# Six groups of an inverse transform as pairs of 64-row tiles, with their evictions and the work behind them in a new order

## The chip, the core and the metric

One core of a Trainium2 chip runs the whole program in one launch. The metric is device time in microseconds (us), the median of several executions. A core has TensorE (PE, matrix products, with a queue of its own for weight loads, PEld), VectorE (DVE), ScalarE (ACT), GpSimd (POOL) and SyncE (SP, which issues most of the transfers here). Each works through its own instructions in order and waits for the others by semaphores. Products land in PSUM, which only DVE and ACT empty in this kernel.

## The reference, cut to what matters

```python
def _A_ref(q, k, v, shift_k, ssm_k, ssm_D):       # S = 2048 positions, D = 640 channels
    k_shift = ...                                 # causal 4-tap convolution of k by channel
    kv = k_shift * v
    y = irfft(rfft(kv, 2*S) * rfft(ssm_k, 2*S))[:S]   # long convolution by channel
    y = y + kv * ssm_D
    return q * y
def _B_ref(x, w1, b1, w2):                        # F = 1728
    h = x @ w1 + b1
    return (h * tanh(softplus(h))) @ w2           # mish
x = A_q
h = x + _A_ref(layernorm(x), A_k, A_v, A_shift_k, A_ssm_k, A_ssm_D)
out = h + _B_ref(layernorm(h), B_w1, B_b1, B_w2)
```

Everything is in bfloat16, with accumulation in float32. `B_x` is not used.

## The kernel before, in words

**The stages.** The long convolution is computed with transforms written as matrix products, in two stages forward (`s1`, `s2`), a product of the two spectra on DVE (`pr`), and two stages back (`i1`, `i2`). The channels come in five blocks `dc` of 128. The first inverse stage has 20 groups, `i1pe{dc}_{gi}`. One group is 16 matmuls (L479): for each of eight sub-blocks two accumulating products, whose stationary operand is a 128x128 piece of the spectrum product `KS`, and whose moving operand is one of two 128x128 constant matrices `a12`. A group fills one PSUM tile of 128x1024 float32 (two banks; there are four such tiles, numbered 0 to 3), and `i1ev{dc}_{gi}` empties it into `Z` (L483) with one cast, on ACT or DVE. The stationary piece is read, and its place in `ks` is free, when the group's matmuls are done.

The second inverse stage takes, for each tile `t` of 128 positions out of 16, four matmuls over `Z` (`i2pe{t}`; for tiles 0 to 3 split into `i2a{t}` over blocks 0 to 3 and `i2b{t}` over block 4). `y{t}` casts the result (128x640) into `tt_s[t]`, a slice of `ks`. Then come, by tile:

- `ln1_{t}` on DVE (bn_stats twice, bn_aggr once) and `ln1p{t}` on POOL (three small instructions, L515 to L517): mean and deviation of the input row; `lnx{t}` (ACT or POOL, L524) normalises it. None of these needs the transforms.
- `wb{t}` (DVE, L538): y times the normalised input; `h{t}` (DVE, L540): plus the input; `bn{t}` (DVE) and `pow{t}` (POOL, L549 and L550): statistics of h; `hc{t}` (DVE, L559): normalised h.
- a transpose of `hc{t}`: by PE for tiles 0 and 1 (`trpe{t}`, L569, then a copy `trev{t}` on ACT), by a transposing transfer on SP for the other tiles (`tr{t}`, L573).

The feed-forward part runs in five units of 256, 256, 512, 512 and 512 positions: unit 0 is tiles 0 and 1, unit 1 tiles 2 and 3, unit 2 tiles 4 to 7, unit 3 tiles 8 to 11, unit 4 tiles 12 to 15. `m1pe{u}_{fp}` (L598, L605) is a seventh of the first product of unit u and needs the transposes of all of its tiles; `hb{u}_{fp}` (ACT) applies mish; `m2pe{t}` (L663, L671) is the second product of tile t, `res{t}` (DVE) adds h, and `d_out{t}` (SP) writes the tile out. L671 is a pair of products of 64 rows each, one on the upper and one on the lower half of the array, with results in two PSUM tiles.

**What sets the order.** All operations are emitted in the order of one hand-written list, `ORDER`. A name with `@n` is a product and the PSUM tile that it writes; `:a`, `:d` and `:p` choose ACT, DVE or POOL where there is a choice (an `i1ev` or `y` without a letter runs on ACT, an `lnx` too). There is no other scheduler: each engine gets its instructions in the order of the list, and waits are put in where data, or a place in a buffer, need them.

**Places.** `ks` holds both halves of `KS`: columns 0 to 20479 and 20480 to 40959, each half with 4096 columns a block. In the second half lie, later on, `w2` (9600 columns from 20480) and the slices `tt_s[t]` (640 columns each, from 30720). `d_w2a`, `d_w2b` and `d_w2c` on SP load `w2`; `w2z` (POOL) zeroes two half chunks of it.

Of the kernel before, what the change touches and what calls it, by code (L numbers as in the profile page):

```python
# [44 lines left out]
pr0_0 s2v1pe_32@0 s2v1ev_0 pr3_64 i1pe1_3@2 d_w14 s2v1ev_64 d_w10 i1pe0_2@3 pr3_96 d_w11 s2v1ev_32 d_w12 i1pe0_1@1 pr4_0 d_w13 i1ev1_3 d_t2m i1pe3_3@0
i1ev0_1 pr2_96 i1pe3_1@2 i1ev3_3 pr2_64 i1pe3_0@1 i1ev0_2 i1pe0_3@0 pr2_0 i1ev3_0 i1pe0_0@3 pr2_32 i1ev3_1 i1pe3_2@1 i1ev0_3 pr4_96 i1pe2_0@2 i1ev0_0
pr4_32 i1pe1_0@0 i1ev2_0 i1pe2_2@3 pr4_64 i1ev1_0 i1pe2_1@2 ln1_8 i1ev3_2 i1pe2_3@0 i1ev2_2 ln1_6 ln1p8 i1pe4_3@1 i1ev2_3 ln1_11 i1pe4_0@3 ln1p6
i1ev2_1 i1ev4_3:d i1pe4_2@0 i1ev4_0 lnx6:p i1pe4_1@2 ln1_4 i1ev4_2 ln1p11 i2a1@1 d_w2a i1ev4_1 ln1_14 i2a0@3 d_w2b ln1p4 d_w2c i2b1 ln1_10 i2a2@0 y1
i2b0 i2pe4@2 y0 wb1 i2pe5@1 y4 h1 i2pe8@3 wb0 y5 h0 i2b2 i2a3@2 y8 bn1 i2pe15@1 y2 i2b3 i2pe12@3 bn0 y15 pow1 i2pe13@0 y3 i2pe11@1 pow0 y12 hc1 wb2
trpe1@2 y11 i2pe7@3 hc0 y13 h2 trpe0@1 trev1:a wb3 i2pe6@0 bn2 trev0:a i2pe10@2 y7 m1pe0_3@1 h3 lnx11 pow2 bn3 m1pe0_2@3 y6 hc2 y10 pow3 ln1_7  # L50
m1pe0_1@0 tr2 lnx8 ln1p10 hc3 hb0_3 m1pe0_5@2 wb8 tr3 hb0_2 h8 ln1p7 m1pe0_6@1 ln1_9 hb0_5 m1pe0_4@3 hb0_1 ln1p14 ln1_15 m1pe0_0@2 hb0_6 lnx4 wb6 w2z
m1pe1_0@0 wb11 lnx10 wb4 lnx7:p hb0_4 m1pe1_4@1 ln1_5 ln1p15 hb1_0 m1pe1_5@3 wb7 hb0_0 h4 ln1p5 hb1_4 m1pe1_3@0 bn8 hb1_5 lnx5:p m1pe1_1@2 ln1_13
hb1_3 pow8 m1pe1_2@1 wb5 hb1_1 h6 ln1p9 lnx15 m1pe1_6@3 bn6 hb1_2 h5 i2pe9@0 pow6 hb1_6 bn4 i2pe14@2 lnx9 ln1p13 m2pe0@1 hc6 ln1_12 y9 tr6 y14 lnx13:p
bn5 lnx14 pow4 hc8 h11 pow5 tr8 m2pe1@3 wb14 h7 ln1p12 hc5 hc4 bn7 tr4 lnx12 wb10 pow7 tr5 bn11 m2pe2@0 h10 pow11 bn10 wb13 pow10 hc7 hc11 tr7 wb9
wb15 m2pe3@2 res0 tr11 h9 hc10 d_out0 h14 tr10 h15 res2 bn9 d_out2 m1pe2_3@1 wb12 pow9 bn14 h12 pow14 m1pe2_6@0 hc9 hb2_3 bn15 tr9 hc14 h13 m1pe2_5@1
tr14 hb2_6 bn12 res3 pow12 m1pe2_4@0 res1 d_out3 hb2_5 pow15 hc12 bn13 tr12 m1pe3_0@2 hc15 pow13 hb2_4 tr15 hc13 d_out1 tr13 m1pe2_0@3 hb3_0 m1pe3_2@1
hb2_0 m1pe3_6@0 hb3_2 m1pe2_1@2 hb3_6 m1pe3_5@3 hb2_1 m1pe2_2@1 hb3_5 m1pe3_1@0 hb2_2 m1pe3_3@2 hb3_1 m1pe3_4@3 hb3_3 m2pe4@1 hb3_4 m2pe6@0 m2pe5@2
res4 res6 d_out6 d_out4 m2pe7@3 m1pe4_2@1 res7 res5 d_out7 d_out5 m1pe4_5@0 m1pe4_6@3 hb4_5 hb4_2 m1pe4_4@2 hb4_6 m1pe4_3@0 hb4_4 m1pe4_0@1 hb4_3
m1pe4_1@3 hb4_0 m2pe9@2 hb4_1 m2pe11@0 m2pe8@1 res11 res9 d_out9 d_out11 m2pe10@3 m2pe15a@0 res10 res8 d_out8 m2pe12@2 res15a d_out15a d_out10
m2pe14@3 m2pe13@1 res14 res12 d_out14 d_out12 m2pe15b@0 res13 d_out13 res15b d_out15b  # L60
# [109 lines left out]
def kernel(  # L170
# [88 lines left out]
    def ev(e, o, i):  # L259
        if e == "act":  # L260
            nc.scalar.copy(o, i)  # L261
        else:
            nc.vector.tensor_copy(o, i)  # L263
# [204 lines left out]
    d_t2m = load("d_t2m", t2m_a, dram["t2m"][:, 0:4096], deps=s1v_in(0, 4096))  # L468
    Z = uv[:].rearrange("p (c j n) -> p c j n", c=NDC, n=P)
    for dc in range(NDC):  # L470
        for gi in range(4):
            p_ = pt()

            def pe(e, gi=gi, p_=p_, dc=dc):
                pz = p_.f32().rearrange("p (g n) -> p g n", g=8)
                for dgl in range(8):
                    b, l = dc * 8 + gi * 2 + dgl // 4, dgl % 4
                    for k in range(2):
                        nc.tensor.matmul(pz[:, dgl, :], KS[:, k, b, :, l], a12[:, k, :], start=k == 0, stop=k == 1)  # L479
# [254 lines left out]
```

## Time and profile before

| | |
|---|---|
| time, median of 3 runs | 225.13 us (225.12 to 225.89) |
| span of the profiled execution (first to last instruction) | 223.5 us |
| busy share of PE, DVE, ACT, POOL in that span | 96%, 60%, 59%, 26% |
| granted PE clock | full, throughout |

The span is the profiled execution's own time as far as the profile has it: it gives no other. The 1.6 us between the span and the median lie before the first and behind the last instruction of the engines. In what follows, times within the span count from its start. A row of the timeline merges like instructions that follow one another; its columns are start, time covered, engine, line, operation, result and operands, count, and in brackets the idle time before it and what ended it. Where a row of the chain of waits names a transfer as the releaser, it was inferred from the times.

### The profile page before, as it was taken

To read this page: it belongs to the slowest core of one execution; us is meant where nothing else is said; L and a number is where in the kernel's file an instruction comes from. 1 tells how busy PE (TensorE), PEld (TensorE's weight loads), DVE (VectorE), ACT (ScalarE), POOL (GpSimd) and SP (SyncE) were. 2 spreads that over 40 slices of the span, in tenths; PEclk is the share of its full clock that TensorE was granted. 3 is DMA by queue.
4 is the path that set the end of the run, shared out by engine and by line. 5 is a ranking of instruction groups with operands and counts; after the bars stand their busy time and mean duration, and the time that the engine had idled before them with its cause. 6 is when DMAs were issued, how large, how long until landed. Compare 5 with 4: busy or idle time off the path is not lost.

```text
span 223.5 us, 6119 instructions
## 1 busy us (share of the span) xinstructions
PE 214.0 (96%) x2645; PEld 157.6 (70%) x2650; DVE 133.2 (60%) x232; ACT 133.0 (59%) x182; POOL 58.9 (26%) x120
## 2 busy tenths in 40 slices
PE   7899999999879999889999999999999999999994
PEld 2899999888869999458877644444567444766763
DVE  2776899999989999889878999100002200022122
ACT  2389888999999999999983015565600075200000
POOL 5147620102860005347887523100000000000000
PEclk9999999999999999999999999999999999999999
DMA  5999994372991789303004443500001100010211
GB/s 181 390 413 409 412 374 121 143 239 93 375 415 69 258 331 290 124 0 62 1 0 62 84 123 91 118 0 0 3 0 59 59 3 0 0 56 6 76 54 49
DMA packets 19563, 30.98 MB, mean 139 GB/s; under 512 B 10704, under 2 KB 14928, under 8 KB 18768
## 3 DMA queue, kind: packets, MB, share of 16 engines
q1 hardware_dynamic: 19104, 30.46, 39.0%
q8 instruction: 21, 0.34, 0.7%
q10 hardware_dynamic: 336, 0.12, 0.2%
q14 instruction: 6, 0.05, 0.1%
q0 software_dynamic: 96, 0.00, 0.0%
HBM read 20.42 MB, written 2.62 MB: 103 GB/s over the span
## 4 chain that ended last, share of the span: by engine, by line
PE 70%; DVE 13%; DMA 9%; ACT 4%; issue 2%; SPq 1%; POOL 1%; DVEq 0%
PE ps L663 26%; PE ps L598 25%; DVE ks L461 6%; DMA ks<-in_B_w_dram 4%; DMA ks<-ks 3%; PE ps L396 3%; PE ps L422 3%; ACT uv L261 3%; DMA ks<-in_A_ssm_k_dram 3%; PE ps L341 2%; PE ps L376 2%; DVE ks L263 2%; PE ps L357 2%; DVE ra L362 1%; PE ps L397 1%
## 5 line engine op out<-in xcount | busy, mean ns | idle before, releaser
L620 ACT ACTIVATE ks<-ps,b1s 128x512 bf16<-128x512 f32 (+1 forms) x69 | 36.1, 610 | 42.8 <-PE ps L598 30.3
L663 PE MATMUL ps<-ks 128*128 128x320 bf16 (+2 forms) x420 | 58.4, 299 | 0.0
L598 PE MATMUL ps<-G 128*128 128x512 bf16 (+1 forms) x320 | 57.0, 336 | 0.3
L688 DVE TENSOR_TENSOR rb<-ps,rb 128x640 bf16<-128x640 f32 x15 | 11.7, 816 | 68.9 <-PE ps L671 66.5
L663 PEld LDWEIGHTS <-ks 128*128 128x128 bf16 x420 | 40.6, 98 | 17.2 <-issue 1.3
L598 PEld LDWEIGHTS <-G 128*128 128x128 bf16 x325 | 31.3, 98 | 24.4 <-issue 1.1
L261 ACT CAST uv<-ps 128x1024 bf16<-128x1024 f32 x49 | 45.2, 1197 | 0.0
L261 ACT CAST ks<-ps 128x960 bf16<-128x960 f32 (+3 forms) x49 | 39.8, 905 | 8.1 <-PE ps L397 5.0
L461 DVE TENSOR_TENSOR ks<-ks,uv 128x2048 bf16<-128x2048 bf16 x20 | 23.1, 1225 | 0.7 <-DMA ks<-ks 0.7
L422 PEld LDWEIGHTS <-G 128*128 128x128 bf16 x512 | 20.9, 96 | 3.1 <-issue 2.5
L479 PE MATMUL ps<-a_t,ks 128*128 128x128 bf16 x320 | 18.8, 219 | 0.4 <-DVE ks L461 0.3
L479 PEld LDWEIGHTS <-ks 128*128 128x128 bf16 x320 | 18.3, 113 | 0.7 <-DVE ks L461 0.6
L422 PE MATMUL ps<-uv,G 128*128 128x64 bf16 (+1 forms) x384 | 12.8, 186 | 1.8 <-ACT uv L261 1.8
L544 DVE BATCH_NORM_STATS2 st<-rb 128x6 f32<-128x320 bf16 x32 | 14.0, 478 | 0.1
L515 POOL TENSOR_SCALAR ve<-mv 128x1 f32<-128x1 f32 x16 | 4.7, 292 | 34.9 <-DVE mv L511 34.2
L510 DVE BATCH_NORM_STATS2 st<-rb 128x6 f32<-128x320 bf16 x32 | 13.7, 471 | 0.0
L263 DVE CAST uv<-ps 128x1024 bf16<-128x1024 f32 x11 | 12.9, 1204 | 0.1
L362 DVE TENSOR_TENSOR ra<-ps,rb 128x1024 bf16<-128x1024 f32 x10 | 11.9, 1222 | 0.7 <-PE ps L358 0.5
L524 POOL TENSOR_SCALAR ra<-rb,r,nmr 128x640 bf16<-128x640 bf16 x8 | 8.9, 1118 | 10.0 <-PE ps L397 9.3
L422 PE MATMUL ps<-ks,G 128*128 128x160 bf16 x128 | 11.2, 230 | 0.0
L396 PE MATMUL ps<-cst,ra 128*64 128x128 bf16 x160 | 10.6, 219 | 0.7 <-ACT uv L261 0.5
L263 DVE CAST ks<-ps 128x1024 bf16<-128x1024 f32 (+1 forms) x9 | 10.5, 1197 | 0.5 <-PE ps L422 0.3
...
## 6 DMA issues: line engine op xcount, KB each, us to landing
...
```

The lines of the kernel that those rows point to most:

```text
L261: nc.scalar.copy(o, i)
L263: nc.vector.tensor_copy(o, i)
L362: nc.vector.tensor_tensor(kv_w[:, m, :, 8 * h:8 * h + 8, :], p_.f32().rearrange("p (l t d) -> p d t l", l=4, t=8), raw_v[:, 8 * h:8 * h + ...
L396: nc.tensor.matmul(ps[0:64, dgl, :], lhs, mc, start=True, stop=True)
L422: nc.tensor.matmul(p_.f32()[:, o:o + n], g_v[:, f, :], src[:, :, f, :], start=True, stop=True)
L461: nc.vector.tensor_tensor(o, o, v, ALU.mult)
L479: nc.tensor.matmul(pz[:, dgl, :], KS[:, k, b, :, l], a12[:, k, :], start=k == 0, stop=k == 1)
L510: nc.vector.bn_stats(st1[:, t, hh, :], xt(t)[:, hh * 320:(hh + 1) * 320])
L544: nc.vector.bn_stats(st2[:, t, hh, :], xt(t)[:, hh * 320:(hh + 1) * 320])
L598: nc.tensor.matmul(ph[:, o:o + w], w1[:, dc, fc * P:fc * P + P], lt[:, dc, 0:w], start=dc == 0, stop=dc == NDC - 1)
L620: nc.scalar.activation(hb[:, fc, 0:n], p_.f32()[:, i * 512:i * 512 + n], ACT.Mish, bias=b1s[:, fc:fc + 1], scale=1.0)
L663: nc.tensor.matmul(p_.f32()[:, o:o + n], lhs, w2[:, k, cols:cols + n], start=fc == 0, stop=single and fc == 13)
```

## The change

Three things change together.

1. The constant tables are laid out anew, so that the 128 rows of a piece of `KS` fall into two halves of 64 that belong to different channels (two channels out of four each). `a12` then has two 64x64 blocks on its diagonal and zeros elsewhere. For the six groups of `ROW_I1` a matmul of 128 rows by 128 moving columns becomes two of 64 rows by 64 columns, one on each half of the array, which write to the two banks of the group's PSUM tile: 32 matmuls and 32 weight loads in place of 16 and 16. All 20 casts `i1ev` read PSUM in runs of two numbers in place of four.
2. `w2` and the slices `tt_s` change places: `tt_s` now lies where blocks 0, 1 and half of 2 were, `w2` where half of 2, 3 and 4 were. Loading `w2` then needs the last groups of block 4 to be done.
3. `ORDER` is new from the last products `pr` on. The casts of groups 2_1, 4_2, 2_3 and 4_3 go to DVE (before, only that of 4_3). `i1pe1_0` moves behind the groups 2_2 and 2_1, and the order of the last groups is new. The six `ln1` that stood between and behind the last casts (tiles 4, 6, 8, 10, 11, 14) move behind `hc2`, and `y0` goes to DVE. Of the `lnx` from tile 4 on, those of tiles 4, 5, 7, 8, 11, 13 and 15 are on POOL (before 5, 6, 7 and 13), and those of 6, 9, 10, 12 and 14 on ACT. `w2z` moves ahead of `pow1`. The units' tiles come in the order 5, 7, 6, 4, then 8, 10, 9, 11, then the rest; the seven `m1pe2` come ahead of all `m1pe3`; `m2pe15a` is now last but one. Elsewhere PSUM tiles 2 and 3 only swap names.

```diff
+ROW_I1 = "2_1 2_3 4_0 4_1 4_2 4_3".split()
...
-    T["g"] = np.moveaxis(G, 4, 6).reshape(128, 128 * 128)
+    T["g"] = G.reshape(2, 16, 4, 128, 2, 16, 2, 2).transpose(0, 1, 2, 3, 6, 5, 7, 4).reshape(128, 128 * 128)
...
-    a12 = np.stack([np.moveaxis(A1, 0, 2).reshape(128, 128), np.moveaxis(A2, 0, 2).reshape(128, 128)], axis=1)
+    a12 = np.zeros((2, 64, 2, 2, 64))
+    for h in range(2):
+        a12[h, :, :, h] = np.stack([np.moveaxis(a, 0, 2).reshape(64, 64) for a in (A1, A2)], axis=1)
...
-    w2 = ks[:, 20480:20480 + 15 * D].rearrange("p (c d) -> p c d", c=15)
-    tt_s = [ks[:, 30720 + t * D:30720 + (t + 1) * D] for t in range(NT)]
+    w2 = ks[:, 30720:30720 + 15 * D].rearrange("p (c d) -> p c d", c=15)
+    tt_s = [ks[:, 20480 + t * D:20480 + (t + 1) * D] for t in range(NT)]
...
-                pz = p_.f32().rearrange("p (g n) -> p g n", g=8)
+                row = f"{dc}_{gi}" in ROW_I1
+                pz = p_.f32().rearrange("p (h g n) -> p h g n" if row else "p (g h n) -> p h g n", h=2, g=8)
                 for dgl in range(8):
                     b, l = dc * 8 + gi * 2 + dgl // 4, dgl % 4
                     for k in range(2):
-                        nc.tensor.matmul(pz[:, dgl, :], KS[:, k, b, :, l], a12[:, k, :], start=k == 0, stop=k == 1)
+                        for r in [slice(0, 64), slice(64, 128)] if row else [slice(0, 128)]:
+                            o = pz[:, r.start // 64, dgl, :] if row else p_.f32()[:, dgl * P:(dgl + 1) * P]
+                            nc.tensor.matmul(o, KS[r, k, b, :, l], a12[r, k, r], start=k == 0, stop=k == 1)
...
-                ev(e, Z[:, dc, :, gi * 32:gi * 32 + 32].rearrange("p j (g l) -> p j g l", l=4), p_.f32().rearrange("p (g j l) -> p j g l", g=8, l=4))
+                ev(e, Z[:, dc, :, gi * 32:gi * 32 + 32].rearrange("p j (g h l) -> p j g h l", h=2, l=2), p_.f32().rearrange("p (h g j l) -> p j g h l" if f"{dc}_{gi}" in ROW_I1 else "p (g h j l) -> p j g h l", h=2, g=8, l=2))
```

The list from the last products to the first product of unit 0, before:

```
pr4_96 i1pe2_0@2 i1ev0_0
pr4_32 i1pe1_0@0 i1ev2_0 i1pe2_2@3 pr4_64 i1ev1_0 i1pe2_1@2 ln1_8 i1ev3_2 i1pe2_3@0 i1ev2_2 ln1_6 ln1p8 i1pe4_3@1 i1ev2_3 ln1_11 i1pe4_0@3 ln1p6
i1ev2_1 i1ev4_3:d i1pe4_2@0 i1ev4_0 lnx6:p i1pe4_1@2 ln1_4 i1ev4_2 ln1p11 i2a1@1 d_w2a i1ev4_1 ln1_14 i2a0@3 d_w2b ln1p4 d_w2c i2b1 ln1_10 i2a2@0 y1
i2b0 i2pe4@2 y0 wb1 i2pe5@1 y4 h1 i2pe8@3 wb0 y5 h0 i2b2 i2a3@2 y8 bn1 i2pe15@1 y2 i2b3 i2pe12@3 bn0 y15 pow1 i2pe13@0 y3 i2pe11@1 pow0 y12 hc1 wb2
trpe1@2 y11 i2pe7@3 hc0 y13 h2 trpe0@1 trev1:a wb3 i2pe6@0 bn2 trev0:a i2pe10@2 y7 m1pe0_3@1 h3 lnx11 pow2 bn3 ...
```

And after, to the transposes of unit 2:

```
pr4_96 i1pe2_0@3 i1ev0_0
i1pe2_2@0 i1pe2_1@2 pr4_32 i1ev2_0 i1ev3_2 pr4_64 i1ev2_2 i1pe1_0@3 i1pe4_2@1 i1ev2_1:d i1ev1_0 i1ev4_2:d i1pe2_3@0 i1ev2_3:d i1pe4_1@2 i1pe4_3@3
i1ev4_3:d i1ev4_1 i1pe4_0@1 i2a0@2 i1ev4_0 i2a1@0 i2b1 i2b0 i2a2@1 y1 i2b2 i2pe4@3 y0:d wb1 i2pe5@0 i2a3@2 wb0 y2 h1 i2b3 w2z h0 y4 bn1 bn0 i2pe6@1 y5
y3 y6 pow1 wb2 i2pe15@3 i2pe7@0 pow0 hc1 d_w2a i2pe13@2 y15 wb3 hc0 y13 h2 i2pe10@1 bn2 y7 h3 bn3 pow2 pow3 d_w2c i2pe11@3 hc2 tr2 ln1_6 hc3 trpe1@2
ln1_5 ln1_4 ln1_8 ln1p6 y11 i2pe12@0 ln1_7 ln1p5 trev1:a trpe0@3 lnx5:p ln1_10 ln1_15 i2pe8@2 trev0:a y12 y10 m1pe0_4@3 wb5 hb0_4 m1pe0_1@0 hb0_1
m1pe0_6@1 ln1_11 ln1p4 m1pe0_3@3 tr3 ln1p7 d_w2b ln1_13 h5 y8 lnx4:p m1pe0_2@0 hb0_6 ln1_9 ln1p8 wb4 lnx7:p hb0_3 wb7 lnx6 m1pe0_0@2 wb6 bn5 hb0_2 h4
hb0_0 h6 lnx8:p m1pe0_5@1 h7 ln1p15 ln1p11 m1pe1_1@3 bn4 m1pe1_4@0 lnx11:p pow5 wb8 hb0_5 m1pe1_2@2 ln1p9 hb1_1 m1pe1_0@1 hb1_4 wb11 bn7 hb1_2 hb1_0
ln1_14 ln1p10 m1pe1_5@3 m1pe1_3@0 hc5 m1pe1_6@2 i2pe9@1 hb1_5 hb1_3 pow7 bn6 i2pe14@3 pow6 h8 pow4 hc7 tr5 hb1_6 lnx15:p y9 m2pe0@0 bn8 y14 hc6
m2pe1@2 pow8 wb15 tr7 lnx9 hc4 wb9 ln1_12 lnx10 m2pe3@1 tr6 ln1p12 tr4 m2pe2@3 ...
```

More of the change, by code (lines that the diff above doesn't have):

```diff
@@ L45 @@
[L45 to L60, printed above, removed]
+sw2_0 s1vev4_0 s1vev3_3:d sw2_1 s1vpe4_2@0 lnx2:p s1vev4_2 s2v0pe_96@3 pr1_64 ln1p3 s2v0pe_16@2 s2v0ev_96 s2v2pe_32@0 s1vev2_3:d lnx3:p s2v0ev_16
@@ new lines @@
+m1pe0_6@1 ln1_11 ln1p4 m1pe0_3@3 tr3 ln1p7 d_w2b ln1_13 h5 y8 lnx4:p m1pe0_2@0 hb0_6 ln1_9 ln1p8 wb4 lnx7:p hb0_3 wb7 lnx6 m1pe0_0@2 wb6 bn5 hb0_2 h4
+hb0_0 h6 lnx8:p m1pe0_5@1 h7 ln1p15 ln1p11 m1pe1_1@3 bn4 m1pe1_4@0 lnx11:p pow5 wb8 hb0_5 m1pe1_2@2 ln1p9 hb1_1 m1pe1_0@1 hb1_4 wb11 bn7 hb1_2 hb1_0
+ln1_14 ln1p10 m1pe1_5@3 m1pe1_3@0 hc5 m1pe1_6@2 i2pe9@1 hb1_5 hb1_3 pow7 bn6 i2pe14@3 pow6 h8 pow4 hc7 tr5 hb1_6 lnx15:p y9 m2pe0@0 bn8 y14 hc6
+m2pe1@2 pow8 wb15 tr7 lnx9 hc4 wb9 ln1_12 lnx10 m2pe3@1 tr6 ln1p12 tr4 m2pe2@3 wb10 res3 res0 ln1p14 h11 h9 lnx14 res1 lnx12 bn9 h10 hc8 bn10 ln1p13
@@ new lines @@
+bn11 lnx13:p m1pe2_6@1 pow10 wb13 wb14 m1pe2_2@0 pow11 h13 hb2_2 hc10 wb12 h14 pow9 hc9 hc11 tr8 bn13 h12 bn14 m1pe2_3@2 tr10 hb2_6 m1pe2_4@0
+m1pe2_0@1 d_out0 res2 bn12 pow13 h15 hb2_3 m1pe2_5@2 tr11 tr9 hb2_4 bn15 pow12 m1pe2_1@0 m1pe3_5@3 hb2_5 pow15 m1pe3_3@2 d_out1 hc13 hb2_0 m1pe3_2@1
+hb3_5 hc15 hb3_2 m1pe3_0@3 pow14 tr13 hb3_0 m1pe3_6@1 hc12 hb3_6 hc14 m1pe3_1@3 m1pe3_4@1 hb2_1 hb3_4 d_out3 tr15 tr12 m2pe5@0 hb3_1 m2pe7@1 tr14
+m2pe4@3 res7 res5 m2pe6@1 m1pe4_2@0 res4 m1pe4_5@3 res6 hb4_2 m1pe4_4@1 d_out2 d_out7 hb4_4 m1pe4_1@0 hb4_5 m1pe4_6@1 hb3_3 m1pe4_3@3 hb4_1 m2pe9@2
@@ L61 @@
+d_out5 hb4_3 d_out6 m2pe8@0 m1pe4_0@3 hb4_6 m2pe11@1 hb4_0 res11 m2pe12@3 d_out4 m2pe14@1 res9 m2pe10@2 res12 m2pe13@3 res14 res13 d_out12 d_out14
+res10 m2pe15a@1 m2pe15b@3 d_out9 d_out13 d_out10 d_out11 res15a res8 d_out15a res15b d_out8 d_out15b
 """.split()
+ROW_I1 = "2_1 2_3 4_0 4_1 4_2 4_3".split()
 CHUNKS = [[0, 1], [2], [3, 4]]
@@ L144, in _make_tables @@
         G[1, :, dl, :, 1, :, dl] = -c
-    T["g"] = np.moveaxis(G, 4, 6).reshape(128, 128 * 128)
+    T["g"] = G.reshape(2, 16, 4, 128, 2, 16, 2, 2).transpose(0, 1, 2, 3, 6, 5, 7, 4).reshape(128, 128 * 128)
     th = 2 * np.pi * g[:, None] * t2[None, :] / 16
     cg, sg = np.cos(th), np.sin(th)
-    A1 = np.zeros((2, 16, 4, 2, 16, 4))
-    A2 = np.zeros((2, 16, 4, 2, 16, 4))
-    for dl in range(4):
+    A1 = np.zeros((2, 16, 2, 2, 16, 2))
+    A2 = np.zeros((2, 16, 2, 2, 16, 2))
+    for dl in range(2):
         A1[0, :, dl, 0, :, dl] = cg
```

7 lines of the change are left out of this document (4 added, 3 removed).

## The prediction

> **What bounds the kernel now.** I read the table of windows first, cut at the end of the last spectrum product (84.7), the start of the first `y` (about 91.2) and the start of unit 0 (99.5).
>
> ```profile
> 84.70:91.20 6.50, 5.74 (x92) 5.10 (x90) 6.33 (x18) 6.45 (x8) 4.34 (x12) 1.00 1.04 343
> 91.20:99.50 8.30, 7.72 (x63) 4.51 (x63) 7.17 (x19) 7.99 (x14) 2.63 (x6) 1.00 0.03 6
> 99.50:220.60 121.10, 120.78 (x819) 75.11 (x821) 46.73 (x115) 45.20 (x82) 26.15 (x57) 1.00 0.16 40
> ```
>
> Columns: stretch, length, busy time of PE, PEld, DVE, ACT, POOL, then clock and DMA. From 99.5 on PE is busy 120.78 of 121.10 us at full clock, and the change adds or takes no product there. So the end can move by what unit 0's start moves, by any gap that opens later, and by the tail. The stretch from 84.7 to 99.5 decides. Its rows in the timelines of PE, ACT and DVE:
>
> ```profile
> 72.87 16.70 PE L479 MATMUL ps<-a_t,ks 128*128 128x128 bf16 x288
> 91.20 5.33 PE L531 MATMUL ps<-uv,ra 128*128 128x128 bf16 x40 [0.77 <-ACT uv L261]
> 98.11 0.45 PE L569 MATMUL ps<-ident,rw 128*128 128x128 bf16 x5 [0.31 <-DVE rw L559]
> 99.49 14.35 PE L598 MATMUL ps<-G 128*128 128x256 bf16 x130
> ...
> 55.23 35.92 ACT L261 CAST uv<-ps 128x1024 bf16<-128x1024 f32 x39
> 91.51 6.66 ACT L261 CAST ks<-ps 128x640 bf16<-128x640 f32 x11 [0.36 <-DMA ks<-in_B_w_dram]
> 97.94 1.43 ACT L261 COPY G<-ps 128x640 bf16<-128x640 bf16 x2
> ...
> 65.28 19.39 DVE L461 TENSOR_TENSOR ks<-ks,uv 128x2048 bf16<-128x2048 bf16 x17 [0.69 <-DMA ks<-ks]
> 87.61 1.18 DVE L263 CAST uv<-ps 128x1024 bf16<-128x1024 f32 x1
> 88.71 0.88 DVE L510 BATCH_NORM_STATS2 st<-rb 128x6 f32<-128x320 bf16 x2
> 92.31 0.49 DVE L538 TENSOR_TENSOR ks<-ks,ra 128x640 bf16<-128x640 bf16 x1 [0.49 <-ACT ks L261]
> 92.83 0.49 DVE L540 TENSOR_TENSOR rb<-ks,rb 128x640 bf16<-128x640 bf16 x1
> 93.24 0.48 DVE L538 TENSOR_TENSOR ks<-ks,ra 128x640 bf16<-128x640 bf16 x1
> 94.17 0.88 DVE L544 BATCH_NORM_STATS2 st<-rb 128x6 f32<-128x320 bf16 x2
> 95.21 0.83 DVE L544 BATCH_NORM_STATS2 st<-rb 128x6 f32<-128x320 bf16 x2
> 97.61 0.45 DVE L559 TENSOR_SCALAR rw<-rb,mv,r 128x640 bf16<-128x640 bf16 x1 [0.46 <-POOL r L550]
> ```
>
> Products end at 65.28 + 19.39 = 84.67. ACT casts without a break to 55.23 + 35.92 = 91.15, 0.92 us each; PE's groups also take 16.70 / 18 = 0.93, so the two are matched and ACT ends last. PE then waits 0.77 us for ACT and starts `i2b1` at 91.20, and `y1` follows at 91.51. The row of `y1` names the load of `w2`. I don't take it: `i2b1` is two short products from 91.20, and `y1` can't precede them; load or no load, the cast ending at 91.15 is the limit. From there the path is y1, wb, h, bn, pow, `hc0` (97.61), its transpose (98.11), the second copy on ACT (97.94 + 1.43 = 99.37), unit 0 (99.49).
>
> **Part 1, the casts.** Behind its last product DVE now runs the four casts that it gets, with no `ln1` ahead. One takes 1.18, and the next instruction started 1.10 behind it (87.61 to 88.71). The first starts at 84.6, the fourth ends at 84.6 + 3 x 1.10 + 1.18 = 89.1. ACT has three casts fewer: 91.15 - 3 x 0.92 = 88.4 if never starved. New runs of two numbers: DVE's PSUM reader with the longest strides (L362, single numbers) and the plain casts cost the same, so I add nothing.
>
> ```profile
> L263 DVE CAST uv<-ps 128x1024 bf16<-128x1024 f32 x11 | 12.9, 1204 | 0.1
> L362 DVE TENSOR_TENSOR ra<-ps,rb 128x1024 bf16<-128x1024 f32 x10 | 11.9, 1222 | 0.7 <-PE ps L358 0.5
> ```
>
> **Part 2, the pairs.** No row shows a pair of 64 by 64. The nearest are L671's pairs of 64 rows in the chain of waits, and the second forward stage, whose moving operand is short (timeline of PE):
>
> ```profile
> 115.70 10.60 PE ps L663 x78
> 126.30 0.38 PE ps L671 x4
> 126.67 3.64 PE ps L663 x26
> ...
> 60.04 1.58 PE L422 MATMUL ps<-uv,G 128*128 128x64 bf16 x48 [0.28 <-ACT uv L261]
> 70.12 2.79 PE L422 MATMUL ps<-uv,G 128*128 128x32 bf16 x96
> ```
>
> A full matmul of L663 takes 10.60 / 78 = 0.136. Four of L671 as two pairs that share the array would be 0.27, one after another 0.54; 0.38 stands there, so they pair, and 0.11 is the change to halves and back. A matmul of 64 columns takes (1.58 less some 0.16 of drain) / 48 = 0.030. Lower bound: a pair costs one such matmul, 16 x 0.030 = 0.47 a group. Upper bounds: each matmul counts by itself, 32 x 0.030 = 0.95, or at the old pace of 0.93 / 16, 1.86. I take 0.47, since L671's rows show sharing, and 0.1 for each of four changes of form.
>
> PE must also wait for PSUM. Group 2_1 and then 1_0 run while the last product ends; 1_0 waits for the cast of 2_0 in its PSUM tile (eight casts ahead of ACT's last before, 91.15 - 8 x 0.92 = 83.8, and unmoved) and leaves PE at 84.8. Group 4_2 runs at 84.9; 2_3 waits for ACT's cast of 2_2 (the second behind 2_0, at 85.7); then 4_1, 4_3, 4_0 follow: 85.7 + 4 x 0.47 + 0.16 of drain = 87.7. DVE wants 4_3 at 87.9 and gets it at 87.3; ACT casts 4_1 and 4_0 by 88.8. DVE is last, at 89.1 in place of 91.15: **2.05 us won**. By the same steps PE takes over from DVE once a group costs over some 0.6, and each 0.1 more costs about 0.4.
>
> **Part 3, from y to unit 0.** `i2b1` starts at 89.15, `i2b0` right behind it, and its result is there by 89.5. `y0` on DVE is bounded by L688, which reads the same PSUM tile in 0.82 (next row): it ends at 90.35, the `y1` of ACT before that. So `wb1` starts at 90.35 against 92.31. The list interleaves wb1, wb0, h1, h0, so that none waits for the one ahead: 4 x 0.41 (from 92.83 to 93.24) = 1.64, against 94.17 - 92.31 = 1.86. `bn1` starts at 92.0, 2.15 earlier than 94.17. From there to `hc0` the steps are the old ones (bn1, bn0, POOL's pow0; wb2, hc1 and wb3 fit into that wait). Behind `hc0` transpose and copy are the same, and ACT has few enough `y` ahead (10 of 0.6 us from 89.5). Unit 0 starts at 99.49 - 2.2 = **97.3**.
>
> ```profile
> L688 DVE TENSOR_TENSOR rb<-ps,rb 128x640 bf16<-128x640 f32 x15 | 11.7, 816 | 68.9 <-PE ps L671 66.5 <-PE ps L663 2.3
> ```
>
> **Part 4, unit 2 in time?** The `ln1` moved out of the old shadow, and three more `lnx` on POOL, now load DVE and POOL while unit 0 runs. What hides them is PE's work up to `m1pe2`, which started at 130.62 and would start at 128.4. It needs `tr4`, the last of unit 2, issued behind `hc4`; ahead of `hc4` in DVE's queue is `wb15`, which waits for POOL's `lnx15`. POOL's rows between 99 and 128, the transposes' landing and unit 2's start:
>
> ```profile
> L550 POOL TENSOR_TENSOR r<-ve,mhalf 128x1 f32<-128x1 f32 x9 | 5.4, 599 | 0.8
> L516 POOL TENSOR_TENSOR r<-ve,mhalf 128x1 f32<-128x1 f32 x8 | 4.9, 618 | 0.7
> L549 POOL TENSOR_SCALAR ve<-mv 128x1 f32<-128x1 f32 x9 | 3.1, 348 | 4.8 <-DVE mv L545 4.5
> L524 POOL TENSOR_SCALAR ra<-rb,r,nmr 128x640 bf16<-128x640 bf16 x3 | 2.6, 867 | 0.2
> L517 POOL TENSOR_SCALAR nmr<-mv,r 128x1 f32<-128x1 f32 x8 | 2.6, 320 | 0.8
> L515 POOL TENSOR_SCALAR ve<-mv 128x1 f32<-128x1 f32 x8 | 2.1, 258 | 0.3
> ...
> G<-rw SPq DMA_TRANSPOSE x9, 2.6
> ...
> 130.62 3.41 PE L598 MATMUL ps<-G 128*128 128x512 bf16 x14
> ```
>
> One `ln1p` takes 0.26 + 0.62 + 0.32 and some 0.22 between, 1.42; a pow 0.35 + 0.60 + 0.09 = 1.04; an `lnx` 0.95. Up to `lnx15` POOL has nine, four and six of them: 12.8 + 4.2 + 5.7 = 22.7 us. It starts when `ln1_6` is done, some 5 us behind `hc0` (two h, two bn of 1.04, `hc2`, `ln1_6`), at 100.4, and ends at 123.1. `wb15` and `hc4` take 0.9, `tr4` lands 2.6 later, at 126.6. DVE's own work in that time (11 `ln1`, 5 bn at 1.04, 12 wb and h at 0.4, 3 hc) is 22.5 us from 99.4, a little less. So 1.8 us are left, and the move costs nothing; without that cover each us past 128.4 would be a us. Unit 3 gains room, since all of `m1pe2` now stands ahead of `m1pe3`.
>
> **Part 5, places and queues.** `d_w2a` now waits for group 4_0 (87.7) in place of 1_0; nothing queues on SP behind it but `tr2`, issued at 99, and `m2pe0` needs `w2` only 16 us after unit 0's start: no cost. `w2z` on POOL finds it idle (2.63 busy of 8.30). The tail:
>
> ```profile
> 215.04 5.51 PE L663 MATMUL ps<-ks 128*128 128x320 bf16 x42
> 220.58 0.42 DVE L685 TENSOR_TENSOR rb<-ps,rb 128x256 bf16<-128x256 f32 x1 [0.70 <-PE ps L663]
> 221.03 0.33 SPq L692 DMA_DIRECT2D out_dram<-rb  x1
> ```
>
> Behind PE's last product come 0.42 and one write. `res8` (0.82) and its write now stand ahead of them; PE's last product takes 5.51 - 28 x 0.136 = 1.7, `res15a` and `res8` by 0.42 for 256 columns and 0.82 some 1.45, so they fit, with 0 to 0.2 lost.
>
> **Sum.** -2.2 of 223.5: a span of 221.3. The median shown lies 1.63 above the span, and I keep that distance: 225.13 - 2.2 = **222.9**. About 0.5% (1.1 us) is what a measurement of this kernel can tell from no change. The forecast's own range is 222.2 (shorter waits, `y0` at less than L688's time) to 223.7 (a group at 0.7).
>
> **Rival A: halves pair, but each short matmul pays its own floor.** Going from 64 to 32 columns saved L422 next to nothing (0.030 to 2.79 / 96 = 0.029), so a floor per instruction is there. If it holds over both halves together, a group is 0.93. Then 4_2 leaves PE at 85.9, the other four at 89.6, the last cast on ACT ends near 90.8; with the 0.15 of part 3, 0.5 is won: 224.6. For it: that floor. Against it: L671's 0.38, though with 320 columns. The Trainium skill, TensorEngine Tiling (Array Packing), section Instruction Overhead, speaks for this rival: about 60 cycles for each matmul on trn2, and no tiling factor is to be taken from a dimension that is already small. By its figure 32 x 60 cycles, at the 2.4 GHz of the skill's page TensorE: Matmul & The Clock Gate (opening table), would be an estimated 0.8 us a group and about 223.9 in the end; no run here shows it for pairs of 64 columns. Chance 0.15, spread from 223.7 to 225.
>
> **Rival B: unit 2 comes late.** POOL's chain of 22.7 us has a slack of 1.8. Single `ln1p` in the rows above vary (idle 1.8 us over eight, by pieces), and DVE and POOL wait for each other. A tenth more is 2.3 us, a gap of 0.5: 223.4. A fifth more is a gap of 2.7: 225.6, slower than before; this is the way to the other side, and from a chain of 26.7 us on (18% over my sum) the whole gain is gone. Chance 0.15, two thirds of it under 224.0.
>
> **Rival C: halves take turns.** If a 64-row matmul keeps the array for the 0.058 of the old pace, five groups in a row cost 9.3 us, the last cast ends near 95.3, 4.15 late, and the time is some 229. The point from which this is slower is about 1.05 a group. L671 speaks against it. With eviction of short runs going slower (L362 speaks against that) chance 0.08.
>
> **How the numbers follow.** Forecast 0.62, A 0.15, B 0.15, C 0.08. Faster by over 0.5% (under 224.0): 0.62 + 0.04 of A + 0.09 of B = 0.75. Within: 0.11 of A and 0.04 of B = 0.15. Slower by over 0.5%: C and 0.02 of B = 0.10. From 222.2 to 225.0 lie nearly all of the forecast and of A and most of B, a little over 0.8.
>
> **What would show it.** Right: L479's 64-row matmuls at about 0.03 a pair; the last `uv` cast on DVE ending near 89.1; L598's first row near 97.3; PE busy without a gap to about 218.4. Wrong: row groups near 0.9 with PE, not DVE, ahead of the last cast (A); an idle time of PE before unit 2's first L598, with a transposing transfer or POOL behind it (B).

## The result, and the profile after

| | before | after |
|---|---|---|
| time, median | 225.27 us (225.12 to 225.89, 4 runs) | 222.97 us (222.90 to 223.17, 4 runs) |
| ratio | | 0.9889, interval 0.9865 to 0.9914 |
| span of the profiled execution | 223.5 us | 221.2 us |

The forecast was 222.9 with a span of 221.3. The table of windows of the changed kernel, cut at the end of the last spectrum product, the start of `i2b1` and the start of unit 0 (columns as before):

```profile
84.50:89.20 4.70, 4.42 (x172) 3.44 (x169) 4.63 (x5) 4.10 (x5) 1.25 (x2) 1.00 0.04 7
89.20:97.16 7.96, 7.79 (x63) 4.66 (x63) 7.25 (x18) 7.48 (x13) 1.76 (x4) 1.00 0.86 278
97.16:218.30 121.14, 120.74 (x817) 75.16 (x820) 52.53 (x132) 43.23 (x79) 33.22 (x71) 1.00 0.17 40
```

The last stretch is as long as before (121.14 against 121.10) and as full, so all of the gain lies ahead of unit 0. The first stretch was 6.5 us long and is 4.7, the second was 8.3 and is 8.0. The timelines of PE, ACT and DVE in them:

```profile
72.88 15.15 PE L485 MATMUL ps<-a_t,ks 128*128 128x128 bf16 x384
88.18 6.87 PE L537 MATMUL ps<-uv,ra 128*128 128x512 bf16 x48 [0.15 <-DVE uv L266]
97.16 14.35 PE L604 MATMUL ps<-G 128*128 128x256 bf16 x130
...
53.43 33.15 ACT L264 CAST uv<-ps 128x1024 bf16<-128x1024 f32 x36
87.00 2.08 ACT L264 CAST uv<-ps 128x1024 bf16<-128x1024 f32 x2 [0.42 <-PE ps L485]
89.55 6.34 ACT L264 CAST ks<-ps 128x640 bf16<-128x640 f32 x10 [0.47 <-PE ps L537]
...
64.84 19.66 DVE L464 TENSOR_TENSOR ks<-ks,uv 128x2048 bf16<-128x2048 bf16 x17 [0.25 <-DMA ks<-ks]
84.42 4.75 DVE L266 CAST uv<-ps 128x1024 bf16<-128x1024 f32 x4
89.73 0.82 DVE L266 CAST ks<-ps 128x640 bf16<-128x640 f32 x1 [0.56 <-PE ps L537]
90.47 0.88 DVE L544 TENSOR_TENSOR ks<-ks,ra 128x640 bf16<-128x640 bf16 x2
92.08 0.88 DVE L550 BATCH_NORM_STATS2 st<-rb 128x6 f32<-128x320 bf16 x2
95.37 0.45 DVE L565 TENSOR_SCALAR rw<-rb,mv,r 128x640 bf16<-128x640 bf16 x1
```

DVE's four casts follow its last product without a break and end at 84.42 + 4.75 = 89.17; ACT's last ends at 87.00 + 2.08 = 89.08, where it ended at 91.15 before. From the last cast to unit 0 it is 7.99 us in place of 8.34: `wb1` to `bn1` takes 1.61 in place of 1.86, and the other steps are within 0.15 of what they were. Unit 0 starts at 97.16 in place of 99.49.

A ruler for what follows. In every run there is one row of PE that the change does not reach, the last 96 matmuls of the second forward stage; it starts at 70.12 before and at 70.13 after. From its start to unit 0's start it is **29.37 us before and 27.03 after, 2.34 less**. This leaves out small offsets from the start of an execution, which single profiles have (up to 0.8 us below).

### The profile page after: what moved, and what is told of

It is laid out like the page before. It is cut to its first block, busy times and chain, and to the rows that moved or that the text cites. A ratio compares the mean times of both kernels' runs of the same rounds, so it can differ in the third digit from the quotient of the medians.

```text
span 221.2 us, 6309 instructions
## 1 busy us (share of the span) xinstructions
PE 212.5 (96%) x2740; PEld 156.0 (71%) x2746; DVE 137.6 (62%) x236; ACT 127.9 (58%) x175; POOL 62.0 (28%) x123
## 4 chain that ended last, share of the span: by engine, by line
PE 72%; ACT 12%; DVE 6%; DMA 5%; issue 2%; SPq 1%; DVEq 0%; ACTq 0%
PE ps L669 26%; PE ps L604 26%; ACT uv L264 9%; PE ps L537 3%; DMA ks<-ks 3%; PE ps L399 3%; PE ps L425 3%; DMA ks<-in_A_ssm_k_dram 3%; PE ps L344 2%; PE ps L379 2%; DVE ks L266 2%; ACT ks L264 2%; PE ps L360 2%; DVE ra L365 1%; DVE uv L266 1%
## 5 line engine op out<-in xcount | busy, mean ns | idle before, releaser
L669 PEld LDWEIGHTS <-ks 128*128 128x128 bf16 x420 | 40.6, 98 | 17.4 <-issue 1.3
L264 ACT CAST ks<-ps 128x960 bf16<-128x960 f32 (+3 forms) x48 | 39.3, 896 | 8.3 <-PE ps L400 5.0
L264 ACT CAST uv<-ps 128x1024 bf16<-128x1024 f32 x46 | 42.6, 1157 | 0.5 <-PE ps L485 0.4
L485 PE MATMUL ps<-a_t,ks 128*128 128x128 bf16 (+1 forms) x416 | 17.1, 208 | 0.4
L485 PEld LDWEIGHTS <-ks 128*128 128x128 bf16 (+1 forms) x416 | 16.5, 114 | 1.0 <-issue 0.4
L266 DVE CAST uv<-ps 128x1024 bf16<-128x1024 f32 x14 | 16.4, 1210 | 0.2
L530 POOL TENSOR_SCALAR ra<-rb,r,nmr 128x640 bf16<-128x640 bf16 x11 | 12.5, 1133 | 9.9 <-PE ps L400 9.3
L266 DVE CAST ks<-ps 128x1024 bf16<-128x1024 f32 (+2 forms) x10 | 11.3, 1160 | 1.0 <-PE ps L537 0.6
L528 ACT ACTIVATE ra<-rb,nmr,r 128x640 bf16<-128x640 bf16 x5 | 4.5, 925 | 11.9 <-POOL nmr L523 11.9
```

Of the source, the lines that this page charges most:

```text
L485: nc.tensor.matmul(o, KS[r, k, b, :, l], a12[r, k, r], start=k == 0, stop=k == 1)
L669: nc.tensor.matmul(p_.f32()[:, o:o + n], lhs, w2[:, k, cols:cols + n], start=fc == 0, stop=single and fc == 13)
```

## The experiments

| kernel | time, us | ratio to before, interval | ruler, us |
|---|---|---|---|
| before | 225.27 | | 29.37 |
| after | 222.97 | 0.9889 (0.9865 to 0.9914) | 27.03 |
| pairs alone | 225.28 | 0.9992 (0.9974 to 1.0010) | 29.37 |
| places alone | 226.15 (one run) | | 29.37 |
| after, no pairs | 225.12 | 0.9994 (0.9976 to 1.0013) | 28.37 |
| after, casts back on ACT | 224.85 | 0.9984 (0.9957 to 1.0011) | 29.00 |
| after, halves in turn | 224.53 | 0.9963 (0.9951 to 0.9976) | 28.65 |
| after, `y0` on ACT | 223.24 | 0.9905 (0.9884 to 0.9925) | 27.34 |
| after, `ln1_6` ahead | 223.11 | 0.9900 (0.9880 to 0.9920) | 27.32 |
| after, all groups as pairs | 226.61 | 1.0050 (1.0031 to 1.0069) | 31.88 |

Four more runs, on what comes behind unit 0, stand at the end.

**The pairs alone.** Tables and `ROW_I1` of the changed kernel, list and places of the kernel before.

```diff
 (before)
+ROW_I1 = "2_1 2_3 4_0 4_1 4_2 4_3".split()
+... the tables, the matmuls and the casts' runs as in the change
```

> The kernel before, with its own order and places, and only the new tables and the six groups as pairs. Theory: ACT's row of casts up to 91.15 is the bound and doesn't get shorter, so the time is that of before, 225.2 (225.0 to 225.4), with PE idle between the groups. Rival (PE is the bound of the stage): six groups shorter by 0.4 each, 2.4 us, so 222.8 or so.

Measured: 225.28 us. The timeline of PE in this run:

```profile
70.24 2.79 PE L425 MATMUL ps<-uv,G 128*128 128x32 bf16 x96
87.65 0.72 PE L485 MATMUL ps<-a_t,ks 64*128 64x64 bf16 x32 [0.20 <-ACT uv L264]
88.57 0.72 PE L485 MATMUL ps<-a_t,ks 64*128 64x64 bf16 x32 [0.20 <-ACT uv L264]
99.61 1.58 PE L604 MATMUL ps<-G 128*128 128x256 bf16 x13
```

A group is done in 0.72, and the next starts 0.92 behind it, when ACT frees its PSUM tile. A faster PE meets the casts' pace and gains nothing. The new tables and the runs of two numbers cost nothing either.

**The new order without the pairs.**

```diff
 (after)
-ROW_I1 = "2_1 2_3 4_0 4_1 4_2 4_3".split()
+ROW_I1 = []
```

> The kernel after, with all 20 first inverse groups as full 128-row products (ROW_I1 empty); order, places and casts as after. Theory (DVE's casts set the end of the stage only because pairs let PE feed them): five full groups of 0.93 behind the last product end on PE near 89.6, the last cast near 90.8 in place of 89.2, unit 0 starts some 1.5 us later (98.7 in place of 97.2), time 224.5 (224.2 to 224.8). Rival (the gain comes from casts and order alone, PE has room): time within 0.3 of 222.97.

Measured: 225.12 us, above the range of the theory. PE's windows (here instructions of L485 alone: PE, PEld, clock, DMA share), its timeline and ACT's:

```profile
87.40:88.30 0.90, 0.90 (x20) 0.90 (x18) 1.00 0.04 9
...
88.51 1.01 ACT L264 CAST uv<-ps 128x1024 bf16<-128x1024 f32 x1 [1.14 <-PE ps L485]
90.29 1.01 ACT L264 CAST uv<-ps 128x1024 bf16<-128x1024 f32 x1 [0.78 <-PE ps L485]
...
70.91 2.79 PE L425 MATMUL ps<-uv,G 128*128 128x32 bf16 x96
99.28 1.91 PE L604 MATMUL ps<-G 128*128 128x256 bf16 x16
107.03 7.27 PE L604 MATMUL ps<-G 128*128 128x256 bf16 x65 [0.50 <-DMA G<-rw]
```

In the stage itself the theory holds: PE needs 0.90 for a group, both casting engines now wait for it (ACT as shown, DVE 0.34 twice), and the ruler is 28.37, so the pairs are worth 1.34 in this order and the rest of the change 1.00 without them. The miss comes later: at 107.03 PE waits 0.50 us for unit 1's transposes, a wait that neither the kernel before nor the changed one has. In all it is 31.80 us from unit 0 to unit 2's first product in this run, against 31.13 in both of those. What makes those transposes late is shown under the last experiment.

**The casts back on ACT.**

```diff
 (after)
-... i1ev2_1:d ... i1ev4_2:d ... i1ev2_3:d ...
+... i1ev2_1 ... i1ev4_2 ... i1ev2_3 ...
```

> The kernel after, with the casts of groups 2_1, 4_2 and 2_3 on ACT again (4_3 stays on DVE). Theory: ACT has three casts more, three times 0.92, and ends near 91.2 in place of 89.1; 2.0 us later, time 225.0 (224.7 to 225.3). Rival (the pairs bring the gain whoever casts): within 0.4 of 222.97.

Measured: 224.85 us. The timeline of PE:

```profile
69.91 2.79 PE L425 MATMUL ps<-uv,G 128*128 128x32 bf16 x96
90.08 3.15 PE L537 MATMUL ps<-uv,ra 128*128 128x512 bf16 x21 [1.11 <-ACT uv L264]
98.91 2.34 PE L604 MATMUL ps<-G 128*128 128x256 bf16 x20
```

PE is done with the groups early and waits 1.11 us for ACT. Of the 2.34 only 0.37 is left. With the run before: the change without the three shared casts brings 0.37, without the pairs 1.00, with both 2.34. Each of the two removes one of two matched limits, PE and the casts.

**Halves in turn.** The same 32 matmuls of a group, in another order: first the 16 of the upper half, then the 16 of the lower.

```diff
 (after)
-for dgl in range(8):
-    for k in range(2):
-        for r in [slice(0, 64), slice(64, 128)]: ...
+for r in [slice(0, 64), slice(64, 128)]:
+    for dgl in range(8):
+        for k in range(2): ...
```

> The kernel after, with the 32 matmuls of a pair group in another order: all 16 of the upper 64 rows, then all 16 of the lower, so that no two neighbours may share the array. Theory (the short group comes from two halves at work at once, 0.033 a pair): a group takes 32 x 0.030 to 0.033, 0.95 to 1.07, as rival A of the prediction had it; the last cast near 91, time 224.7 to 225.4. Rival (what shortens a group is the number of columns, whatever the neighbours; or the queue brings halves together): 222.97 within 0.3.

Measured: 224.53 us, just under the theory's range. A window of one group in the changed kernel and one in this run (L485 alone), then this run's timeline of PE:

```profile
86.25:86.78 0.53, 0.53 (x43) 0.53 (x39) 1.00 0.00 0
```

```profile
87.65:88.51 0.86, 0.86 (x39) 0.86 (x37) 1.00 0.00 0
...
69.97 2.79 PE L425 MATMUL ps<-uv,G 128*128 128x32 bf16 x96
98.62 2.56 PE L604 MATMUL ps<-G 128*128 128x256 bf16 x22
```

(The counts include matmuls that run over the window's edge.) A group of pairs takes 0.53 us, 0.033 a pair; in turn it takes 0.86, 0.027 a matmul (0.95 to 1.07 was expected for the group). So of the two orders only the one with neighbours on different halves lets the halves work at the same time, and this alone is worth 1.62 of the 2.34. Whether the matmuls themselves or their weight loads are what runs side by side, these two runs don't separate. The price in turn is close to what rival A had for pairs. By the Trainium skill, TensorEngine Tiling (Array Packing), Instruction Overhead, 60 cycles for each matmul made an estimated 0.8 us a group. That agrees with the matmuls in turn (0.86) and not with the pairs (0.53), which behave as if each half paid it by itself.

**`y0` on ACT, and `ln1_6` ahead of `y0`.** Two steps of part 3 undone, one at a time.

```diff
 (after, y0 on ACT)
-y0:d
+y0
 (after, ln1_6 ahead)
-i1ev4_3:d i1ev4_1 ... hc2 tr2 ln1_6 hc3
+i1ev4_3:d ln1_6 i1ev4_1 ... hc2 tr2 hc3
```

> The kernel after, with y0 on ACT in place of DVE. Theory: ACT, which casts y without a break up to the copy of the transposes, gets one more cast of 0.6 ahead of both copies, and DVE wins nothing as wb0 needs y0 anyway; unit 0 starts 0.4 to 0.6 later, time 223.4 to 223.6. Rival (ACT has room there, DVE is the path): DVE has 0.75 less ahead of wb1, time 222.3 to 222.9.

> The statistics of the next tile (ln1_6, three VectorE instructions of about 1.0 together) stand again among the casts at the end of the inverse's first stage, as in the kernel before, behind the last cast that VectorE has there and ahead of y0; all else is as in the changed kernel. Theory: VectorE idles 0.57 ahead of y0 in the changed kernel, so 1.0 there makes y0 and, behind it, wb1, bn1 and unit 0 later by about 0.4: 223.2 to 223.6. Rival: y0 isn't on the path to unit 0 and the statistics are hidden: 222.7 to 223.1.

Measured: 223.24 and 223.11 us. By the ruler, which is 0.31 and 0.29 longer, both directions are right and both sizes too large. The medians are 0.27 and 0.14 longer, which is inside the intervals, and both lie below the theories' ranges, the second at the edge of its rival's. With `y0` on ACT, `wb1` starts no later than in the changed kernel, but ACT's copies of the transposes end later; with `ln1_6` ahead, DVE's idle 0.56 us in front of `y0` takes up half of it.

**The places alone.**

```diff
 (before)
-    w2 = ks[:, 20480:...]   tt_s = [ks[:, 30720 + t * D:...] ...]
+    w2 = ks[:, 30720:...]   tt_s = [ks[:, 20480 + t * D:...] ...]
```

> The kernel before, with only w2 and the slices tt_s changing places, so that the load of w2 waits for group 4_1 (about 89.5 in place of 83.4) and lands 8 us later, near 98. Theory (the first y waits for the second inverse product and not for w2, as the prediction said against the chain's row): time as before, 225.2 within 0.4. Rival (the row is right, y1 waits for the load): y1 near 98 in place of 91.5, time 231 or so.

Measured: 226.15 us in a single run, 0.55 above the theory's range and far from the rival's 231. Its timelines of PE, SP and ACT, and its row of transfers (size, time to landing):

```profile
70.64 2.79 PE L422 MATMUL ps<-uv,G 128*128 128x32 bf16 x96
100.01 1.25 PE L598 MATMUL ps<-G 128*128 128x256 bf16 x10
...
90.06 0.39 SPq L491 DMA_DIRECT2D ks<-in_B_w_dram  x1
...
92.04 6.66 ACT L261 CAST ks<-ps 128x640 bf16<-128x640 f32 x11 [0.36 <-PE ps L531]
...
ks<-in_B_w_dram SPq DMA_DIRECT2D x1, 2080.0 KB, 9.5
```

The load of `w2` is issued at 90.06 and lands 9.5 us later, yet `y1` casts at 92.04, as far behind the last `uv` cast as before. So `y1` does not wait for the load, whatever the chain of waits of the kernel before names there. The ruler is unchanged to 0.01; 0.52 of the excess lies ahead of the ruler's start, where the edit touches nothing, and one run can't say more.

**All groups as pairs.**

```diff
 (after)
-ROW_I1 = "2_1 2_3 4_0 4_1 4_2 4_3".split()
+ROW_I1 = [f"{dc}_{gi}" for dc in range(5) for gi in range(4)]
```

> All twenty groups of the inverse's first stage run as pairs, where the changed kernel has six. Theory: from its third group on this stage is set by the casts out of PSUM and not by the products (in the changed kernel PE already waits between groups once a group costs 0.53), so fourteen more groups that are some 0.35 shorter on PE give nothing: 222.7 to 223.3, PE's busy time some 5 lower. Rival: PE also sets the pace of the first fourteen groups, and each gives its part of 0.35 less on the path: 220 or below. Second rival: a pair costs more where the operands were just written (the six were a lucky choice): above 224.

Measured: 226.61 us, slower than the kernel before. The number agrees with the second rival, but not its reason: a group of pairs costs what it did (0.72 with its drain). None of the theories had what the profile shows. The chain of waits of PE between 66 and 92 (sum, times, longest), a row of its timeline, and one of its windows:

```profile
PE ps L485 <- issue: 4.6, 3, 2.2
...
82.01 3.28 PE L485 MATMUL ps<-a_t,ks 64*128 64x64 bf16 x127 [2.16 <-issue]
...
81.25:84.66 3.41, 2.65 (x100) 2.65 (x102) 3.20 (x3) 2.24 (x3) 0.00 (x0) 0.50 0.59 245
```

PE stands still three times, 4.6 us together, each time inside a group, where it waits for no other engine (the first time between the 26th and the 27th matmul of one). The changed kernel has no such break in that stretch. During the first one the granted clock falls to 0.50 and stays there for 3.41 us, and it does so once more behind the third. Data transfers can't be the reason for all three: they fill the DMA engines in the first break (their share is 1.08 from 79.85 to 81.25), but not in the other two. The trace points at the arrival of PE's own instructions. From break to break there are 128 matmuls and as many weight loads (of the first 128 matmuls one record is missing), and a transfer of 16 KB on the DMA queue that the profile calls `instruction` comes, on the mean in each kernel here, once for 244 to 250 recorded instructions of PE. In this stretch these transfers end at 80.63, 84.81 and 88.48, and PE goes on 1.4 to 1.6 us behind each. PE has 448 more instructions in this stage, so that they would come too late. No run changed this delivery, so it stays an inference from times that fit.

**Unit 2's slack.** `lnx15` is issued three times, and five times, on GpSimd (each time the same result), which puts some 2 and some 4 us more into POOL's chain ahead of unit 2.

```diff
 (after)
-nc.gpsimd.tensor_scalar(lnx_s[t % 9], xt(t), ...)
+for _ in range(3 if t == 15 else 1):      # 5 in the second kernel
+    nc.gpsimd.tensor_scalar(lnx_s[t % 9], xt(t), ...)
```

> The kernel after, with lnx15 on POOL done three times (the same result written again), which puts 1.9 us into POOL's chain ahead of wb15, hc4 and the last transpose of unit 2. Theory (that chain has a slack of 1.8 to 1.9: its transpose is issued at 123.78 and lands 2.6 later, unit 2 starts at 128.3): 223.0 to 223.4. Rival (no slack was left, or one of many us): 224.9, or no change with a transpose landing well ahead of unit 2.

> The kernel after, with lnx15 on POOL done five times, 3.8 us more in the chain ahead of the last transpose of unit 2. Theory: 1.9 of it is hidden and 1.9 to 2.3 shows as an idle time of PE ahead of unit 2's first product, time 224.8 to 225.3. Rival (POOL's chain hangs on nothing that ends last): 222.97 within 0.3.

Measured: 224.38 us (224.17 to 225.06; ratio 0.9949, 0.9931 to 0.9966) and 228.45 us (227.65 to 229.53; ratio 1.0137, 1.0095 to 1.0179). Both lie above the expected ranges, by 1.0 and 3.1 us. The changed kernel first (POOL's `lnx15`, DVE's `wb15` and `hc4`, PE's first product of unit 2), then the run with three (the same four):

```profile
122.00 0.87 POOL L530 TENSOR_SCALAR ra<-rb,r,nmr 128x640 bf16<-128x640 bf16 x1
122.91 0.49 DVE L544 TENSOR_TENSOR ks<-ks,ra 128x640 bf16<-128x640 bf16 x1 [0.83 <-POOL ra L530]
123.31 0.44 DVE L565 TENSOR_SCALAR rw<-rb,mv,r 128x640 bf16<-128x640 bf16 x1
128.29 1.25 PE L604 MATMUL ps<-G 128*128 128x512 bf16 x4
```

```profile
123.66 2.83 POOL L531 TENSOR_SCALAR ra<-rb,r,nmr 128x640 bf16<-128x640 bf16 x3
126.53 0.49 DVE L545 TENSOR_TENSOR ks<-ks,ra 128x640 bf16<-128x640 bf16 x1 [2.80 <-POOL ra L531]
126.94 0.44 DVE L566 TENSOR_SCALAR rw<-rb,mv,r 128x640 bf16<-128x640 bf16 x1
130.11 1.24 PE L605 MATMUL ps<-G 128*128 128x512 bf16 x5 [1.31 <-DMA G<-rw]
```

The chain is the one the prediction named: `lnx15`, `wb15`, `hc4`, `tr4`, unit 2. But `lnx15` starts 1.66 us later before any of the added work has run. POOL's chain, from its first `ln1p` of that stretch (100.34 and 100.77), takes 21.66 us to `lnx15` in the changed kernel and 22.89 here, for the same instructions. It is 22.9 in eight of the eleven kernels with the new order, 21.7 in the changed kernel and in that without pairs and `hc4` first, 22.0 with `ln1_6` ahead. So there is a short course and one that is 1.23 longer. The rows of POOL and DVE show how they part, first in the changed kernel, then in the run with three:

```profile
108.98 1.96 POOL L530 TENSOR_SCALAR ra<-rb,r,nmr 128x640 bf16<-128x640 bf16 x2
110.29 1.79 DVE L544 TENSOR_TENSOR ks<-ks,ra 128x640 bf16<-128x640 bf16 x3
```

```profile
109.85 2.67 POOL L531 TENSOR_SCALAR ra<-rb,r,nmr 128x640 bf16<-128x640 bf16 x2
110.69 1.24 DVE L545 TENSOR_TENSOR ks<-ks,ra 128x640 bf16<-128x640 bf16 x3
```

An `lnx` on POOL and a `wb` on DVE hold each other up. In the changed kernel the second `lnx` starts 0.22 ahead of DVE's three products, takes 0.86, and the first product takes 0.99 in place of some 0.45. In the run with three it starts 0.02 behind them and takes 1.81. So a few hundredths decide which engine waits; that these waits are the whole of the 1.23 was not tested.

1.96 of added work and 1.23 less the slack of 1.8 make 1.4, where PE waits 1.31. The run with five adds 3.9: 3.3 by the same sum, and 3.28 measured. Its PE shows what the rest is (timeline, then a window):

```profile
131.56 2.29 PE L605 MATMUL ps<-G 128*128 128x512 bf16 x5 [3.28 <-DMA G<-rw]
...
131.05:134.46 3.41, 2.90 (x13) 1.15 (x15) 3.38 (x8) 1.15 (x2) 2.78 (x8) 0.50 0.00 0
```

After the wait PE gets half its clock until 134.46, and the five matmuls take 2.29 in place of 1.25: 2.9 us of work at half pace cost another 1.45. With 3.28 and 1.45 the changed kernel's 222.97 becomes 227.70, and this execution took 227.65; the others of this kernel took up to 1.9 more. The two longest (229.04 and 229.53) have a mean granted clock of 0.983 and 0.985, the two others 0.992, which is one such stretch of 3.41 us. A second stretch, worth up to 1.7, would explain most of it; no profile shows where it lies.

**`hc4` ahead of `wb15`.** Is it the queue behind `wb15`, or POOL's length as such?

```diff
 (after, lnx15 three times; the same edit in the run without pairs)
-m2pe1@2 pow8 wb15 tr7 lnx9 hc4 wb9
+m2pe1@2 pow8 tr7 lnx9 hc4 wb15 wb9
```

> As the run with lnx15 three times on GpSimd (224.38, PE idle 1.4 ahead of unit 2), with one step moved: VectorE's wb15, which waits for lnx15, stands behind hc4 and no longer ahead of it. Theory: unit 2 was late because hc4, whose own inputs are ready about 2.7 earlier, stood on VectorE behind wb15's wait for lnx15; with hc4 first, tr4 is issued near 124.4, lands near 127.1, ahead of the 128.3 at which PE comes to it, and the time is that of the changed kernel, 222.8 to 223.3. Rival: GpSimd's whole chain is late, pow4 itself or the transposes set unit 2, and the time stays within 0.4 of 224.4.

> As the run of the changed kernel without pairs (225.12, 0.67 more between unit 0 and unit 2 than in the changed kernel), with VectorE's wb15 behind hc4 instead of ahead of it. Theory: that 0.67 was the same wait of hc4 behind wb15, and it goes: 224.2 to 224.7, which is what the six groups' pairs are worth by themselves (1.4 or so). Rival: the 0.67 has another cause (the transposes, or the run): within 0.25 of 225.12.

Measured for the first: 222.78 us (222.73 to 223.80; ratio 0.9888, 0.9867 to 0.9910), 1.60 less than with `wb15` ahead, and as fast as the changed kernel although POOL works 2 us more. The slot of `hc4` behind another instruction's wait was the whole cost. The timelines of DVE and PE, from the slowest of its executions (223.80):

```profile
122.85 1.38 DVE L566 TENSOR_SCALAR rw<-rb,mv,r 128x640 bf16<-128x640 bf16 x2
...
129.12 1.24 PE L605 MATMUL ps<-G 128*128 128x512 bf16 x5 [0.81 <-DVE rb L695]
```

`hc6` and `hc4` now run one behind the other at 122.85. In this execution the wait has moved on: `res`, still behind `wb15`, frees PSUM 0.81 late. The other executions took 222.73 to 223.06 and can hardly have it.

Measured for the second: 225.61 us (225.00 to 226.34; ratio 0.9998, 0.9981 to 1.0016), no gain; the theory fell, and the time is 0.24 above the rival's range too. The loss of the run without pairs is not at unit 2. In both of these kernels PE waits at unit 1, and the transposing transfers there take longer to land. Here are the second kernel's PE row and, for it and then for the changed kernel, the transfers' row between 85 and 109:

```profile
106.65 7.27 PE L604 MATMUL ps<-G 128*128 128x256 bf16 x65 [0.58 <-DMA G<-rw]
...
G<-rw SPq DMA_TRANSPOSE x2, 3.5
```

```profile
G<-rw SPq DMA_TRANSPOSE x2, 2.6
```

They are issued 2.1 us behind unit 0's start in both kernels, so the wait comes from the landing: of the two, the second takes 4.3 us in place of 2.7. Its packets show why. The last 12 of 640 start from 105.24 on, when a 16 KB transfer of the queue `instruction` (104.31 to 105.26) ends; in the first run without pairs it is the last 3, from 105.79 on, and the transfer lasts from 104.86 to 105.81. In the nine other kernels with the new order no such transfer meets the transposes (in the changed kernel it comes from 104.75 on, when both have landed), and they land in 2.6. Without the pairs PE has 192 instructions fewer, and the transfers of instructions fall elsewhere. So the 0.50 and 0.58 that PE waits at unit 1 come from where those transfers happen to fall, and not from the order or from slower products.

## Why the prediction was right

| step | predicted | measured |
|---|---|---|
| a group of pairs | 0.47 | 0.53 |
| last group leaves PE | 87.7 | 88.03 |
| last casts end | DVE 89.1, ACT 88.8 | 89.17, 89.08 |
| `y1`, `wb1`, `bn1` start | 89.5, 90.35, 92.0 | 89.55, 90.47, 92.08 |
| unit 0 starts | 97.3 | 97.16 |
| POOL done with `lnx15` | 123.1 | 122.87 |
| unit 2 starts | 128.4 | 128.29 |
| lost in the tail | 0 to 0.2 | 0 |

**Part 1** holds: four casts, 1.13 to 1.26 apart, no price for runs of two numbers. **Part 2**: the halves share the array, as read from L671's rows; a pair costs 0.033 and not 0.030. That was cheap, since DVE and not PE is last up to some 0.6 a group. The other side of that bend was measured too: at 0.90 a group the ruler is 1.34 longer, where the prediction's 0.4 for each 0.1 over 0.6 gives 1.2. With the halves in turn, at 0.86, it is 1.62 longer where the rule gives 1.0: the size of that slope is only roughly right. **Rival A** had the right price for the wrong order of matmuls, and **rival C** falls: 0.027 for a 64-row matmul even in turn, against the 0.058 that it needs.

**Part 3** is right in sum, to 0.14. **Part 4** is right in this kernel, but too sure of itself: POOL's chain came out at 21.66 to `lnx15`, as summed, in the changed kernel, and 1.23 longer in eight of the ten others, which the bound of "a tenth more" in **rival B** covers. That the sum met the shorter course is luck: the sum has no term for the time that DVE and POOL take from each other. The time did not hang on it: with the casts back on ACT the chain took the longer course, and unit 2 still started 31.13 us behind unit 0. Of the slack of 1.8, some 0.6 is left in the longer course. Rival B's mechanism was shown by adding work. Its sum for the wait holds too: with five `lnx15` the chain runs from 100.25 to 127.94, 27.7 us, which is 5.0 over the sum, less the slack 3.2 (3.28 measured). But this would make 226.2; the 228.45 measured hold a price that the rival lacks, the lower clock behind such a wait. **Part 5** holds: from the end of PE's last matmul to the end of the span it is 3.0 us in both kernels. The chain row that named the load of `w2` was indeed a wrong inference.

What the prediction did not say is how the gain divides: no part brings much alone (pairs 0.00, places 0.00, the order with its casts 1.00 in the stage and nothing measurable in the time), and 1.34 of the 2.34 appear only with both.
